# An earlier x, a later W_out and a finer interleave at the start of a convolution and feed-forward kernel

## The chip, the cores and the metric

One core of one Trainium2 chip. Times are device microseconds (us) of one execution; a kernel's figure is the median of its runs. The span of a profile is some 1.75 us shorter than the time of the same execution. All runs here are with a granted TensorE clock of 0.998 or more.

## The reference, cut

```python
# attention part: softmax over 7 taps per head, causal 7-tap convolution along the sequence
out = np.einsum('hk,bskhg->bshg', w, x_unf)      # x: 8 x 4096 x 192, 8 heads of 24 columns
# feed-forward part on the 32768 rows
h = x @ w_in                                     # 192 -> 2048
g = 0.5 * h * (1.0 + erf(h * inv_sqrt2))         # Gelu
return g @ w_out                                 # 2048 -> 192
```

## The kernel before

The two halves of the tokens go side by side through 35 blocks of columns (six of 256, then 29 of 512). For each block DVE transposes x and convolves it, PE does the first layer, ACT the Gelu, PE the second layer. Blocks 0 and 1 are convolved on PE instead, by products with diagonal matrices ("diagonal products"), and their results are copied out of PSUM. W_in comes in three parts (columns 0 to 255, 256 to 511, 512 to 1023 of each half); DVE copies each part to the other half of the partitions. W_out comes in four pieces, cast by GpSimd (POOL in the profile). In blocks 0 and 1 the first layer goes in eight steps (0 to 7), each followed by one Gelu; steps 4 to 7 of block 0 read the copied halves of W_in. Before any data is in, PE runs 16 "warm-up" products on a constant tile.

The parts that the change and the argument touch:

```python
# SyncE: the queue of all later loads
load(sp, 0, (0, 1))            # block 0's x (the other half of it goes on ACT's queue)
sp.wait_ge(S_WIN[0], 32)       # W_in's first part is in
load(sp, 1)                    # block 1's x
for i in range(4):
    ...                        # W_out, four pieces of 384 KB
load(sp, 2)                    # block 2's x
load(sp, 3)
...
# GpSimd: W_in's parts on its own queue; halos; casts of block 1's x; then
for i in range(4):
    g.wait_ge(S_WOUT[i], 16)
    g.tensor_copy(wout[...], woutf[...]).then_inc(S_WOG)      # cast of a piece of W_out
...
# DVE
for p in range(NP): trans(0, p)
conv_out(v, 0, 1); conv_out(v, 0, 4)      # two of block 0's six result copies
dup(0); dup(1)                            # W_in's parts to the other partitions
for p in range(NP): trans(1, p)           # waits for block 1's x
dup(2)
for j in range(len(PIECES)): conv_out(v, 1, j)    # block 1's six result copies
# then for every block from 2 on: three transposes, 21 convolution steps
...
# PE: diagonal products of block 1, behind first-layer steps 4 and 5 of block 0
behind = {
    (0, 4): [(1, kd, k) for k in taps for kd in (0, 1)],
    (0, 5): [(1, kd, k) for k in taps for kd in (2, 3)],
}
```

## Time and profile before

| | before |
|---|---|
| median of the first three runs | 683.88 us (683.34 to 684.79) |
| span of the profile, PE busy in it | 681.6, 675.0 us |
| block 1's x in, transposed from | 12.39, 12.41 us |
| last part of W_in in, last piece of W_out in | 10.70, 18.17 us |
| block 2's x in, transposed from | 19.62, 19.65 us |
| block 1 and block 2: first weights of the first layer | 18.01, 29.15 us |

Landings are the last of the 16 to 64 landing records of a transfer. SyncE's queue in order of time, with the start and length of a group of issues:

```profile
6.53 1.82 SPq L329 DMA_DIRECT2D xin<-in_x_dram  x4
8.39 2.10 SPq L878 DMA_DIRECT2D woutf<-in_moe_w_out_dram  x4
10.53 8.72 SPq L329 DMA_DIRECT2D xin<-in_x_dram  x12
```

W_in alone moves 139 GB/s.

### The profile page before, as it was taken

The page shows a single profiled execution, that of the slowest core. Times are in us where ns is not written, and L with a number is a line of the kernel's source. Part 1 is how long each engine was busy: PE and PEld are TensorE (multiplying, and loading weights), DVE is VectorE, ACT ScalarE, POOL GpSimd, SP SyncE. Part 2 cuts the span into 40 slices and gives each one's busy share as a digit, 9 for nine tenths or more (in the row PEclk, how much of TensorE's full clock was granted, in tenths as well). Part 3 has the DMA queues.
Part 4 walks back from the last instruction along what each step waited for, and adds up shares of the span by engine and source line. Part 5 has one row for each costly group of instructions (what it writes and reads, how often), then busy time and mean ns, then how long its engine had stood idle before and what let it go on. Part 6 is the DMA issues. An engine that isn't in the chain of part 4 may idle for free.

```text
span 681.6 us, 27317 instructions
## 1 busy us (share of the span) xinstructions
PE 675.0 (99%) x12576; PEld 410.1 (60%) x12576; DVE 561.0 (82%) x904; ACT 537.3 (79%) x550; POOL 38.9 (6%) x57
## 2 busy tenths in 40 slices
PE   8999999999999999999999999999999999999998
PEld 4899655555555555555555555555555555555556
DVE  6899979888889888899888898888898888988611
ACT  6899988787787777787777788777878777878772
POOL 5026000000000000000000000000000000000000
PEclk9999999999999999999999999999999999999999
DMA  9446323234332244332244422334322434310123
GB/s 222 86 101 134 79 60 75 43 75 95 96 94 58 45 91 94 95 86 47 60 94 95 94 69 46 78 94 96 94 52 46 95 94 96 83 42 21 48 49 94
DMA packets 132994, 54.79 MB, mean 80 GB/s; under 512 B 126480, under 2 KB 132752, under 8 KB 132880
## 3 DMA queue, kind: packets, MB, share of 16 engines
q1 hardware_dynamic: 130960, 51.50, 32.5%
q8 instruction: 98, 1.61, 1.0%
q0 software_dynamic: 1248, 0.79, 0.9%
q10 hardware_dynamic: 672, 0.76, 0.4%
q14 instruction: 16, 0.13, 0.1%
HBM read 28.66 MB, written 25.17 MB: 79 GB/s over the span
## 4 chain that ended last, share of the span: by engine, by line
PE 96%; ACT 2%; DMA 1%; issue 0%; DVE 0%; SPq 0%; ACTq 0%
PE hp L760 48%; PE ob L824 43%; PE ob L791 6%; ACT gT L681 2%; DMA xin<-in_x_dram 1%; PE ob L711 0%; ACT xc L191 0%; ACT osb L269 0%; DVE osb L311 0%; DVE xT L526 0%; ACT xTb L630 0%; SPq L872 0%; DVE osb L280 0%; SPq L329 0%; ACTq L629 0%
## 5 line engine op out<-in xcount | busy, mean ns | idle before, releaser
L681 ACT ACTIVATE gT<-hp 128x1024 bf16<-128x1024 f32 x512 | 523.3, 1024 | 128.8 <-PE hp L760 125.5
L760 PE MATMUL hp<-xc,win 64*64 64x512 bf16 (+2 forms) x6048 | 419.5, 366 | 1.5 <-ACT gT L681 0.7
L824 PE MATMUL ob<-gT,wout 64*64 64x512 bf16 x5376 | 366.3, 376 | 0.0
L559 DVE SCALAR_TENSOR_TENSOR acc<-xT,wcol,acc 128x512 f32<-128x512 f32 (+1 forms) x495 | 314.1, 698 | 0.0
L760 PEld LDWEIGHTS hp<-xc,win 64*64 64x64 bf16 (+1 forms) x6048 | 189.9, 106 | 134.8 <-ACT gT L681 2.5
L824 PEld LDWEIGHTS ob<-gT,wout 64*64 64x64 bf16 x5376 | 172.3, 118 | 122.8
L311 DVE STREAM_TRANSPOSE osb<-ob 128x512 f32<-128x512 f32 x84 | 74.1, 885 | 100.8 <-PE ob L824 100.8
L526 DVE STREAM_TRANSPOSE xT<-xin 128x512 f32<-128x512 f32 (+1 forms) x105 | 78.6, 797 | 3.8 <-DMA xin<-in_x_dram 3.8
L559 DVE SCALAR_TENSOR_TENSOR xc<-xT,wcol,acc 128x512 bf16<-128x512 f32 (+1 forms) x99 | 65.0, 708 | 0.0
L447 POOL COPY xT<-xT 128x18 f32<-128x18 f32 x30 | 27.9, 930 | 505.2 <-DVE xT L526 482.9
L791 PE MATMUL ob<-wout,gT 64*128 64x192 bf16 x1024 | 52.9, 243 | 0.3
L791 PEld LDWEIGHTS ob<-wout,gT 64*128 64x128 bf16 x1024 | 44.9, 94 | 5.2 <-PE ob L791 0.6
L552 DVE TENSOR_SCALAR acc<-xT,wcol 128x512 f32<-128x512 f32 (+1 forms) x90 | 37.5, 474 | 1.1
L282 ACT ACTIVATE osb<-ob 128x192 f32<-128x192 f32 x4 | 1.3, 332 | 9.5 <-PE ob L791 9.5
L280 DVE COPY osb<-ob 128x192 f32<-128x192 f32 x4 | 1.4, 358 | 8.4 <-PE ob L791 8.4
L695 PE MATMUL hp<-warm 128*128 128x512 bf16 x16 | 5.1, 485 | 1.3 <-DVE warm L463 1.3
L269 ACT ACTIVATE osb<-ob 128x384 f32<-128x384 f32 x12 | 5.8, 486 | 0.0
L654 ACT ACTIVATE acc<-xT,wcol 128x256 f32<-128x256 f32 (+1 forms) x9 | 5.2, 575 | 0.0
L695 PEld LDWEIGHTS hp<-warm 128*128 128x128 bf16 x16 | 1.8, 119 | 4.0 <-issue 1.9
L384 POOL DMA_DIRECT2D win<-in_moe_w_in_dram x6 | 3.9, 658 | 0.8 <-POOLq L905 0.8
L711 PE MATMUL ob<-xTb,dg 64*64 64x256 bf16 (+1 forms) x112 | 3.2, 245 | 0.7 <-ACT xTb L630 0.7
L193 DVE CAST xc<-ob 64x256 bf16<-64x256 f32 (+3 forms) x8 | 2.8, 357 | 1.3 <-PE ob L711 1.1
(31 smaller groups left out, 22.4 us busy)
## 6 DMA issues: line engine op xcount, KB each, us to landing
out_dram<-osb SPq DMA_DIRECT2D x122, 192.0 KB, 3.1
xin<-in_x_dram SPq DMA_DIRECT2D x116, 192.0 KB, 4.1
xin<-in_x_dram SPq DMA_DIRECT2D x20, 96.0 KB, 4.2
woutf<-in_moe_w_out_dram SPq DMA_DIRECT2D x4, 384.0 KB, 6.2
win<-in_moe_w_in_dram POOLq DMA_DIRECT2D x4, 96.0 KB, 4.6
win<-in_moe_w_in_dram POOLq DMA_DIRECT2D x2, 192.0 KB, 5.1
out_dram<-osb SPq DMA_DIRECT2D x8, 48.0 KB, 1.9
out_dram<-osb ACTq DMA_DIRECT2D x4, 96.0 KB, 1.9
```

Source lines behind the costliest of these rows:

```text
L269: e.activation(out=dst, in_=src, func=AF.Copy).then_inc(S_EVA)
L311: v.transpose(ap(osb[m % 2], j, [[8 * C, 128], [C // 2, TB // 32], [NP, 32]]), bank(ring(m, j)),).then_inc(S_EV)
L447: g.tensor_copy(dst, src).then_inc(S_HALO)
L526: v.transpose(ap(xT[n % 2], p * XW + HX, [[NP * XW, 128], [1, w]]), ap(xin[n % NX], p, [[TB // 32 * DQ, 128], [D if n == 0 else DQ, w // 3 ...
L552: ins = v.tensor_scalar(a, src, wk, None, ALU.mult)
L559: ins = v.scalar_tensor_tensor(dst, src, wk, a, op0=ALU.mult, op1=ALU.add)
L654: a.activation(out=acc[n % 2][:, p * TB : p * TB + w], in_=ap(xT[n % 2], p * XW + HX, [[NP * XW, 128], [1, w]]), func=AF.Copy, scale=wcol[ ...
L681: a.activation(out=ap(gT[n % 2], i * c * 2 * w, dst), in_=ap(hp[u % 2], 0, src), func=AF.Gelu,).then_inc(S_GELU)
L695: t.matmul(hp[1][:, 0:512], warm[:, 0:128], warm[:, :])
L760: ins = t.matmul(hp[u % 2][fo : fo + fw, o : o + w], ap(win, f1, [[NP * F, 64], [2, fw]]), xc[n % 2][r, p * TB : p * TB + w], start=(p == ...
L791: ins = t.matmul(bank(bb[sub], w=C), gT[m % 2][r, c0 : c0 + 128], wout[r, CH[sub][i] * C : (CH[sub][i] + 1) * C], start=(ph == 0 and i == ...
L824: ins = t.matmul(bank(ring(m, j), slice(64 * h, 64 * h + 64), w), ap(wout, 64 * hf * NF * C + CH[h][i] * C + j, [[NF * C, 64], [NP, 64]],) ...
```

## The change

Its intent is to have block 1's x early, so that its diagonal products can lie in the slack of block 0's Gelus, and to keep W_out away from the parts of W_in that are needed first.

```diff
@@ DVE @@
-                v.wait_ge(S_WIN[s], 32)
+                v.wait_ge(S_WIN[min(s, 2)], 32)
 ...   (each dup copies a quarter, FQ columns, of a half; before: FQ, FQ, 2 FQ)
+            v.wait_ge(S_TR, NP)
+            v.tensor_copy(<third part of block 0's xTb>, <xT>).then_inc(S_CASTV)
             conv_out(v, 0, 1)
             conv_out(v, 0, 4)
-            dup(0)
-            dup(1)
             for p in range(NP):
                 trans(1, p)
-            dup(2)
-            for j in range(len(PIECES)):
+            for s in range(3):
+                dup(s)
+            for j in range(3):
+                conv_out(v, 1, j)
+            dup(3)
+            for j in range(3, len(PIECES)):
                 conv_out(v, 1, j)
@@ ACT @@
-            for p in range(NP):
+            for p in range(NP - 1):          # casts of block 0's x
@@ PE @@
-                (0, 4): [(1, kd, k) for k in taps for kd in (0, 1)],
-                (0, 5): [(1, kd, k) for k in taps for kd in (2, 3)],
+                (0, 3): [(1, kd, k) for k in taps[:4] for kd in (0, 1)],
+                (0, 4): [(1, kd, k) for k in taps[4:] for kd in (0, 1)],
+                (0, 5): [(1, kd, k) for k in taps[:4] for kd in (2, 3)],
+                (0, 6): [(1, kd, k) for k in taps[4:] for kd in (2, 3)],
 ...   (block 0's products of the third part now wait for S_CASTV)
-                if n == 0 and 4 <= i < 7:
+                if n == 0 and i >= 4:
                     t.wait_ge(S_DUPE, 2 * (i - 4) + 2)
@@ SyncE @@
             load(sp, 0, (0, 1))
-            sp.wait_ge(S_WIN[0], 32)
             load(sp, 1)
+            sp.wait_ge(S_WIN[1], 32)
             for i in range(4):               # W_out
```

More of the change, by code (lines that the diff above doesn't have):

```diff
@@ L148, in bass_lightweight_conv__then__act_gelu_exact_kernel @@
         S_CAST = [sem("S_CAST%d" % i) for i in range(len(PC))]
+        S_CASTV = sem("S_CASTV")
         S_PC = sem("S_PC")
@@ L504, in dup @@
                             win,
-                            64 * (1 - hf) * NP * F + FH + FP[s],
-                            [[NP * F, 64], [F, NP], [1, FP[s + 1] - FP[s]]],
-                        ),
-                        ap(
-                            win,
-                            64 * hf * NP * F + FP[s],
-                            [[NP * F, 64], [F, NP], [1, FP[s + 1] - FP[s]]],
-                        ),
+                            64 * (1 - hf) * NP * F + FH + FQ * s,
+                            [[NP * F, 64], [F, NP], [1, FQ]],
+                        ),
+                        ap(win, 64 * hf * NP * F + FQ * s, [[NP * F, 64], [F, NP], [1, FQ]]),
                     ).then_inc(S_DUPE)
@@ L581, in _ @@
                 trans(0, p)
+            v.wait_ge(S_TR, NP)
+            v.tensor_copy(
+                ap(xTb[0], (NP - 1) * XB + HL, [[NP * XB, 128], [1, WS[0]]]),
+                ap(xT[0], (NP - 1) * XW + HX, [[NP * XW, 128], [1, WS[0]]]),
+            ).then_inc(S_CASTV)
             conv_out(v, 0, 1)
             conv_out(v, 0, 4)
-            dup(0)
-            dup(1)
             for p in range(NP):
                 trans(1, p)
-            dup(2)
-            for j in range(len(PIECES)):
+            for s in range(3):
[4 more added lines that the diff above has]
+            for j in range(3, len(PIECES)):
                 conv_out(v, 1, j)
@@ L700, in pconv @@
                 if k == KS - 1:
-                    t.wait_ge(S_CAST[PC[n]], p + 1)
+                    if n == 0 and p == NP - 1:
+                        t.wait_ge(S_CASTV, 1)
+                    else:
+                        t.wait_ge(S_CAST[PC[n]], p + 1)
                     if n == 0:
```

## The prediction

> **What bounds the kernel now.** I read the page first, for the share of each engine, then the chain that ended last, then the start in order of time, because the diff touches nothing after block 1.
>
> ```profile
> span 681.6 us, 27317 instructions
> PE 675.0 (99%) x12576; PEld 410.1 (60%) x12576; DVE 561.0 (82%) x904; ACT 537.3 (79%) x550; POOL 38.9 (6%) x57
> ...
> PE 96%; ACT 2%; DMA 1%; issue 0%; DVE 0%; SPq 0%; ACTq 0%
> ```
>
> The first lines are the busy times, the last is the chain of waits by engine. PE carries 96% of the chain, so the time can change only by what is not PE: 681.6 - 675.0 = 6.6 us in all, of which 5.93 us pass before the first x is transposed and nothing in the diff shortens that. The whole room of the change is therefore well under 2% (13.7 us).
>
> Next the start in order of time (start, length, engine, line; in brackets the idle time ahead and its releaser), cut to the lines that decide:
>
> ```profile
> 12.41 1.34 DVE L526 STREAM_TRANSPOSE xT<-xin 128x256 f32<-128x256 f32 x3 [1.57 <-DMA xin<-in_x_dram]
> 13.89 0.96 PE L711 MATMUL ob<-xTb,dg 64*64 64x256 bf16 x28
> 15.54 0.59 PE L711 MATMUL ob<-xTb,dg 64*64 64x128 bf16 x28
> 15.65 1.02 ACT L681 ACTIVATE gT<-hp 128x1024 bf16<-128x1024 f32 x1 [0.63 <-PE hp L760]
> 15.81 2.29 DVE L193 CAST xc<-ob 128x256 bf16<-128x256 f32 x6
> 16.93 4.00 ACT L681 ACTIVATE gT<-hp 128x1024 bf16<-128x1024 f32 x4 [0.26 <-PE hp L760]
> 18.22 0.83 POOL L457 CAST wout<-woutf 128x768 bf16<-128x768 f32 x1 [1.25 <-DMA woutf<-in_moe_w_out_dram]
> 19.65 1.35 DVE L526 STREAM_TRANSPOSE xT<-xin 128x256 f32<-128x256 f32 x3 [1.54 <-DMA xin<-in_x_dram]
> 21.82 6.02 DVE L559 SCALAR_TENSOR_TENSOR acc<-xT,wcol,acc 128x256 f32<-128x256 f32 x15
> 27.77 1.26 DVE L559 SCALAR_TENSOR_TENSOR xc<-xT,wcol,acc 128x256 bf16<-128x256 f32 x3
> 29.14 0.58 PEld L760 LDWEIGHTS hp<-xc,win 64*128 64x128 bf16 x12 [0.15 <-issue]
> ```
>
> See three things. (1) From 10.10 to about 18 us ACT's Gelu sets the pace of block 0, and the two lumps of 28 diagonal products put gaps of 0.63 and 0.26 us into it. (2) Block 1's first layer starts at 18.01 us (its weights in the trace), behind a Gelu and behind the six copies that DVE ends at 18.10. (3) Block 2's x lands only at 19.6 us: DVE idles 1.54 us for it, then works without a hole, and its last convolution step ends at 29.03; block 2's first weights load at 29.15. So PE is handed block 2 0.12 us after DVE ends. The stretches from that landing on show DVE full:
>
> ```profile
> 19.65:29.10 9.45, 9.32 (x196) 8.32 (x192) 9.41 (x25) 7.35 (x9) 0.31 (x1) 1.00 0.27 52
> 29.10:39.70 10.60, 10.60 (x228) 10.53 (x225) 10.56 (x28) 9.61 (x14) 0.39 (x2) 1.00 0.34 85
> ```
>
> The columns are the length, then busy time of PE, PEld, DVE, ACT, POOL, the clock, the DMA share and GB/s. DVE is busy 9.41 of 9.45 and 10.56 of 10.60 us: it is as full as PE. I set the end of each block's last convolution step beside the first weight load of that block, from the same trace: block 2 29.03 and 29.15, block 3 39.56 and 39.67, block 4 47.92 and 50.14, block 5 57.33 and 60.66, block 6 69.26 and 71.18, and 2.1 us apart or more from there to the end. So up to 39.7 us the true chain runs: landing of block 2's x, then 19.9 us of DVE work, then PE. The page's chain names PE there because PE is also busy; the two are almost tied, with PE's slack about 0.15 us at block 2 and 0.06 at block 3.
>
> **What the Trainium skill says.** "DMA: Bandwidth & Descriptors", section "Queues, rings and completion order": each DMA engine takes turns between the queues that have work for it, and takes one queue's work in order. The trace agrees: W_in is on POOL's queue, everything else on SP's, W_out's packets come behind block 1's x. The page's "Specifications" table puts line rate at 512 B and up; x's rows here are 384 B packets. The trace shows about 300 of them in 0.5 us (230 GB/s) with two blocks of x in flight, against 350 GB/s while W_out's 1536 B packets run (11.5 to 15.0 us), so it agrees in direction. "Perfetto Trace Analysis", "Identifying the Most-Contended Engine": matmul busy time says little, weight-load busy time more; here PEld is 8.32 of 9.45 us in block 1 and 10.53 of 10.60 in block 2, so it doesn't hide a large hole either. "VectorE: DVE Perf Modes", section "The perf-mode tier table", bears on the one cast moved to DVE; no row of the trace has that very shape.
>
> **The change part by part.**
> The cast of block 0's third part goes from ACT (0.417 us) to DVE, an estimate of 0.3 to 0.4 us from the 0.42 us that a 256-wide copy out of PSUM takes. The part is transposed at 7.26; ACT's cast ended at 7.72, DVE's will at about 7.6. But the first copies of block 0's result start at 8.01 and wait for earlier products. Gain: 0 to 0.1 us.
> The slots: 28 + 28 products become 16, 12, 16, 12 behind the first-layer steps 3 to 6. The lumps took 0.89 and 0.52 us of PE; a slot takes 0.51, 0.38, 0.30, 0.22. A step of 0.66 to 0.83 us plus a slot nearly fits a Gelu of 1.02, so of the 0.89 us of gaps I expect 0.1 to 0.3 to remain. The six copies start at 14.4 instead of 15.8; the last three (0.29 + 0.29 + 0.28) follow the last slot at about 16.4, or W_in's last copy (two of 0.42), and end at 17.4. Block 1 then starts at 17.4 in place of 18.0: 0.6 us gained on PE.
> The copies of W_in's other half: 4 of 0.42 and 2 of 1 us become 8 of 0.42, the same work, now ahead of the wait by need only.
> The orders of transfers: block 1's x is issued at 2.1 us rather than at 6.53, and W_out when W_in's second part is in rather than at 8.39. Bytes are unchanged. Block 1's x lands at some 8 to 10 us instead of 12.39, which the slots need (first one at 12.8).
> What it does to block 2's x decides. Before, between 7.0 and 8.75 us W_in ran alone at 139 GB/s; with x beside it, 8.75 to 11.5, the engines moved 251. So putting x into the earlier stretch saves up to (251 - 139) x 1.75 = 196 KB, an estimate of 0.6 to 0.8 us. Against it, W_out is now issued at 7.6 to 9.2 us (W_in's second part: 31 of 32 engine landings by 7.4 us before, one straggler at 8.71), and its first packets came 2 us after issue. That is 9.7 to 11.2 us, against 10.4 before (but then at half rate until 12). Shift of W_out and hence of block 2's x: between -0.9 and +0.4 us, most likely -0.4.
> Sum: the end moves by the smaller gain of the two chains, min(0.6 + 0.15 on PE, 0.4 on DVE's) = 0.4 us. 683.88 - 0.4 = about 683.5.
>
> **The rivals.**
> A: the PE gain counts in full, 0.6 us or more, 683.2. For it: the page's chain is nearly all PE. Against: the 0.12 us hand-overs at blocks 2 and 3, which swallow what isn't matched by an earlier x.
> B: the gain is lost entirely; block 2's x lands where it did, as the same bytes go through the same engines ahead of it, and PE merely waits longer at 29 us: 683.9. For it: DMA share is 0.94 to 1.45 from 4.5 to 19.65 us. Against: the thin stretch at 7 us.
> C: W_out starts late, a hole opens between W_in's end and W_out's start, and block 2's x comes 0.5 to 1 us late: 684.4 to 684.9. For it: the new wait is on the queue that carries all later x as well, and it hangs on the slowest of 32 landings.
> D: W_in's last part, now sharing with x, lands after 11.2 us, where step 2 needs it (10.70 before), or W_in's first part after 8.85 (6.51 before). Slack 0.5 and 2.3 us; a miss costs PE a few tenths, which the 0.6 us would absorb.
>
> **Range and chances.** I weigh my path 45%, B 25%, C 20%, A 10%; runs of the kernel before already spread from 683.34 to 684.79, and I take that spread to come from landings such as these. Predicted 683.5 us, 8 in 10 between 682.6 and 684.6. More than 2% either way is out of reach of a change that touches 20 us: faster 0.5%, within 2% 98.5%, slower 1%.
>
> **What would show it.** Block 1's transposes before 11 us: x early, right. Gelu gaps of block 0 under 0.3 us and block 1's first layer near 17.4: slots, right. Then block 2's transposes: their start against 19.65 should equal the shift of its last convolution step (29.03), of block 3's hand-over (39.67) and of the end. If the transposes start no earlier and PE has a wait of 0.5 us or more at 29 us, B is right; a start later than 19.8 means C. I'd be wrong at the root if the end moves without the transposes moving, or if the DVE chain has holes after them. If the end moves by over 1 us, the cause lies outside block 2's landing, and I have missed a part.

## More of the kernel before

The columns are the stretch and its length, the busy time of PE, PEld (weight loads), DVE, ACT and POOL, then the clock, the DMA share and GB/s:

```profile
7.00:8.75 1.75, 1.68 (x56) 1.47 (x56) 0.66 (x3) 1.43 (x4) 0.76 (x3) 1.00 0.94 139
13.00:15.00 2.00, 1.87 (x44) 1.41 (x46) 1.94 (x4) 1.99 (x3) 1.98 (x4) 1.00 1.09 383
```

W_out, from 13 to 15 us, moves 383.

## The result, and the profile after

| | before | after |
|---|---|---|
| median, four runs each | 683.71 us (683.34 to 684.79) | 684.69 us (683.96 to 685.62) |
| ratio, 95% interval | | 1.0012 (0.9995 to 1.0030) |
| span of the profile | 681.6 | 683.0 |

A ratio is the mean time of one kernel's runs over that of the other's of the same rounds, so it is not quite the ratio of the medians. The verdict is "same" at 2%, as predicted; the predicted gain of 0.4 us isn't there, and the changed kernel tends to be about 1 us slower. Its median lies 0.09 us above the top of the stated range, the ratio times 683.71 (684.5) just inside.

The page of the changed kernel, busy times and chain:

```profile
span 683.0 us, 27320 instructions
PE 676.3 (99%) x12576; PEld 410.3 (60%) x12576; DVE 562.0 (82%) x907; ACT 536.4 (79%) x549; POOL 38.8 (6%) x57
...
PE 95%; ACT 2%; DVE 1%; DMA 1%; issue 0%; SPq 0%
```

PE's busy time rose by 1.3 us, though it does the same 12576 products. The 16 warm-up products alone take 6.59 us instead of 5.05 (more on them below). The start in order of time:

```profile
9.76 1.94 SPq L887 DMA_DIRECT2D woutf<-in_moe_w_out_dram  x4
10.80 1.34 DVE L523 STREAM_TRANSPOSE xT<-xin 128x256 f32<-128x256 f32 x3 [1.20 <-DMA xin<-in_x_dram]
12.17 3.77 DVE L503 COPY win<-win 64x768 bf16<-64x768 bf16 x6
15.98 1.33 DVE L194 CAST xc<-ob 128x256 bf16<-128x256 f32 x3
17.34 0.87 DVE L503 COPY win<-win 64x768 bf16<-64x768 bf16 x2
18.36 1.49 PE L769 MATMUL hp<-xc,win 64*128 64x256 bf16 x24 [0.73 <-DVE win L503]
19.23 2.98 ACT L685 ACTIVATE gT<-hp 128x1024 bf16<-128x1024 f32 x3 [0.82 <-PE hp L769]
21.07 1.34 DVE L523 STREAM_TRANSPOSE xT<-xin 128x256 f32<-128x256 f32 x3 [2.02 <-DMA xin<-in_x_dram]
30.57 0.47 PEld L769 LDWEIGHTS hp<-xc,win 64*128 64x128 bf16 x10 [0.30 <-issue]
```

Block 1's x is transposed at 10.80 instead of 12.41. But block 2's transposes start at 21.07 instead of 19.65, 1.42 us later, and the span is 1.42 us longer. PE, at block 2, stands idle for 0.30 us. It too is late: the first Gelu of block 0 starts at 10.86 (10.10 before), the fourth pair of W_in copies (17.34) stands behind result copies and holds up first-layer step 7 of block 0, with a Gelu gap of 0.82 us behind it, and block 1 starts at 18.90 instead of 18.01. The stretches of the changed kernel:

```profile
7.00:8.75 1.75, 1.75 (x45) 1.12 (x47) 0.89 (x3) 0.64 (x2) 1.14 (x4) 1.00 1.30 225
13.00:15.00 2.00, 2.00 (x44) 1.30 (x44) 1.94 (x3) 1.75 (x2) 1.60 (x2) 1.00 0.88 232
```

From 7 to 8.75 us the engines move 225 GB/s instead of 139: the gain that the prediction counted on. From 13 to 15 they move 232 instead of 383. In that stretch almost nothing but W_out is on the engines in either kernel: 487 of its packets start before, 292 after, with a median of 0.065 us in both. So most packets are not slower; there are fewer of them. What was won is lost again, and more.

### The profile page after: what moved, and what is told of

Its sections match the earlier page's. It is cut to its first block, busy times and chain, and to the rows that moved or that the text cites. A ratio compares the mean times of both kernels' runs of the same rounds, so it can differ in the third digit from the quotient of the medians.

```text
span 683.0 us, 27320 instructions
## 1 busy us (share of the span) xinstructions
PE 676.3 (99%) x12576; PEld 410.3 (60%) x12576; DVE 562.0 (82%) x907; ACT 536.4 (79%) x549; POOL 38.8 (6%) x57
## 4 chain that ended last, share of the span: by engine, by line
PE 95%; ACT 2%; DVE 1%; DMA 1%; issue 0%; SPq 0%
PE hp L769 47%; PE ob L833 42%; PE ob L800 5%; ACT gT L685 1%; DMA xin<-in_x_dram 1%; DVE win L503 1%; SPq L330 0%; DVE xT L523 0%; DVE xc L194 0%; ACT osb L270 0%; DVE osb L312 0%; SPq L881 0%; DVE osb L281 0%
## 5 line engine op out<-in xcount | busy, mean ns | idle before, releaser
L699 PE MATMUL hp<-warm 128*128 128x512 bf16 x16 | 6.6, 604 | 1.3 <-DVE warm L464 1.3
L503 DVE COPY win<-win 64x768 bf16<-64x768 bf16 x8 | 4.5, 558 | 0.2
```

The source lines that it names most:

```text
L503: v.tensor_copy(ap(win, 64 * (1 - hf) * NP * F + FH + FQ * s, [[NP * F, 64], [F, NP], [1, FQ]],), ap(win, 64 * hf * NP * F + FQ * s, [[NP ...
L699: t.matmul(hp[1][:, 0:512], warm[:, 0:128], warm[:, :])
```

## The experiments

Theory ("chains"): the end is set by the later of two chains, landing of block 2's x plus DVE's work, and PE's own work; both slipped. Rivals for the late landing: W_out released late; chance; DVE's copies or GpSimd's casts disturbing the transfers; the slots. The first table has all results; the second has what the profiles show. Kernels are compared only within the same rounds. "Late" release means W_out behind W_in's second part, "early" behind its first.

| run | edit, against the changed kernel (A) or before (B) | median, before | ratio (95%) |
|---|---|---|---|
| e0 | A again | 684.57, 683.57 | 1.0015 (1.0002 to 1.0027) |
| e1 | A with the transfer order of B | 686.68, 683.57 | 1.0047 (1.0034 to 1.0060) |
| e2 | B with the transfer order of A | 683.62, 683.57 | 1.0000 (0.9988 to 1.0013) |
| e3 | A, fourth W_in copy ahead of block 1's result copies | 684.04, 683.57 | 1.0003 (0.9990 to 1.0017) |
| e4 | A, casts of W_out held until all of it is in | 687.48, 683.91 | 1.0049 (1.0027 to 1.0071) |
| e5 | A, W_in copies cut to 16 columns (wrong result) | 684.95, 683.91 | 1.0015 (0.9998 to 1.0031) |
| e6 | e2 again | 684.60, 683.58 | 1.0016 (1.0002 to 1.0030) |
| e7 | A without the slots | 684.01, 683.58 | 1.0010 (0.9997 to 1.0022) |
| e8 | e3, W_out behind W_in's first part | 684.26, 683.58 | 1.0008 (0.9995 to 1.0020) |
| e9 | e8, casts held as in e4 | 684.78, 683.46 | 1.0012 (0.9998 to 1.0026) |
| e10 | A, W_out behind W_in's first part | 684.10, 683.46 | 1.0006 (0.9993 to 1.0019) |
| e11 | e2, W_out behind W_in's first part | 684.02, 683.46 | 1.0005 (0.9993 to 1.0018) |

| profile | block 1's x | W_out | GB/s, 13 to 15 us | W_out's last piece in | block 2's x in | its transposes | span less that | PE idle ahead of block 2 |
|---|---|---|---|---|---|---|---|---|
| before | second | early | 383 | 18.2 | 19.62 | 19.65 | 661.96 | 0.15 |
| e1 | second | early | 383 | 17.7 | 19.37 | 20.93 | 663.69 | none |
| after | first | late | 232 | 19.9 | 21.04 | 21.07 | 661.97 | 0.30 |
| e0 | first | late | 204 | 19.3 | 20.84 | 20.87 | 661.96 | 0.56 |
| e2 | first | late | 292 | 18.2 | 19.58 | 19.60 | 662.03 | none |
| e3 | first | late | 215 | 20.1 | 21.29 | 21.32 | 661.98 | 0.46 |
| e4 | first | late | 205 | 19.7 | 20.92 | 20.95 | 664.75 | none |
| e5 | first | late | 258 | 20.0 | 21.28 | 21.30 | 661.96 | 0.43 |
| e6 | first | late | 240 | 19.0 | 20.45 | 20.47 | 661.97 | 0.72 |
| e7 | first | late | 243 | 20.1 | 21.37 | 21.40 | 661.97 | 0.54 |
| e8 | first | early | 361 | 15.6 | 18.77 | 19.26 | 663.23 | none |
| e9 | first | early | 366 | 17.9 | 19.49 | 19.52 | 663.57 | none |
| e10 | first | early | 355 | 17.8 | 19.48 | 19.51 | 662.77 | none |
| e11 | first | early | 342 | 15.9 | 19.09 | 19.11 | 663.17 | none |

Read the last three columns first. Wherever PE idles ahead of block 2, the span is the start of block 2's transposes plus 661.96 to 661.98 us, in seven profiles of six kernels. Wherever PE doesn't idle there, the span is longer than that sum: then PE is the later chain (e2 is the tie, 662.03). This holds for every profile, so the end is read off two numbers at 20 to 30 us. (The last column is the idle time of PE's weight loads, as in the line at 30.57 above.)

**e0, the changed kernel again.**

> The changed kernel again, unchanged, for its spread and a second profile. Chain theory (the end is the start of block 2's transposes plus 661.9 us, as 19.65 gave 681.6 before and 21.07 gave 683.0 after): the span of this profile is its own transposes' start plus 661.9 within 0.2. Rival, chance: block 2's x lands anywhere from 19.5 to 21.5 in any run and the mean against before is within 0.3 us. Rival, the order itself: landing again at 20.7 or later and the mean 0.7 to 1.3 us slower than before.

684.57 against 683.57, landing at 20.84, span 682.8 = 20.87 + 661.96. The slower time is there a second time, with an interval that leaves out 1.0. Its spread is wide, though (683.86 to 685.66).

**e1 and e2, one half of the change each.**

```diff
 e1: A with                              e2: B with
-            load(sp, 1)                 -            sp.wait_ge(S_WIN[0], 32)
-            sp.wait_ge(S_WIN[1], 32)                  load(sp, 1)
+            sp.wait_ge(S_WIN[0], 32)    +            sp.wait_ge(S_WIN[1], 32)
+            load(sp, 1)
```

> The changed compute order (slots, split copies, moved cast) with the transfer order of before. If the new transfer order is what delays block 2's x: landing back at about 19.6, end set by the later of DVE chain and PE; x of block 1 is back at 12.4, so the W_in copies on DVE come after it, 12.4 + 1.35 + 6 x 0.45 to 0.9 = 17 or later, and first-layer steps 4 to 7 of block 0 wait for them: PE slow by about 1 to 2 us, total 684.5 to 685.5. If chance alone made the difference: same as before within 0.3.

> The compute order of before with only the new transfer order. If the transfer order is to blame for all: block 2's x lands at 20.7 or later and the end is 0.7 to 1.4 us later than before (684.4 to 685.1). If W_out's late issue is not the cause but the lagging engines are chance: landing near 19.6 on average and the end within 0.3 of before.

e1 was 3.1 us slower than before, twice what I expected. The landing is back, at 19.37, but DVE is free for it only at 20.93, and PE is later still:

```profile
12.64 1.33 DVE L523 STREAM_TRANSPOSE xT<-xin 128x256 f32<-128x256 f32 x3 [3.60 <-DMA xin<-in_x_dram]
14.00 3.81 DVE L503 COPY win<-win 64x768 bf16<-64x768 bf16 x6
15.02 0.83 PE L769 MATMUL hp<-xc,win 64*128 64x256 bf16 x12 [0.31 <-DVE win L503]
20.22 1.49 PE L769 MATMUL hp<-xc,win 64*128 64x256 bf16 x24 [1.14 <-DVE win L503]
```

These lines are from the order of time of e1: DVE idles 3.60 us for block 1's x with all its W_in copies queued up behind, and PE waits for the copies. The new compute order can't do without the early x.

e2 looked the same as before, and its profile had block 2's x at 19.58. Taken alone this says that the new transfer order is harmless and the compute order guilty. It is the one look that misled me; e6 contradicts it.

**e3, the copy that PE waits for moved ahead.**

```diff
-            for s in range(3):
-                dup(s)
-            for j in range(3):
-                conv_out(v, 1, j)
-            dup(3)
-            for j in range(3, len(PIECES)):
-                conv_out(v, 1, j)
+            for s in range(4):
+                dup(s)
+            for j in range(len(PIECES)):
+                conv_out(v, 1, j)
```

> The changed kernel with the fourth W_in copy moved ahead of block 1's result copies, so that first-layer step 7 of block 0 doesn't wait for it behind them. Chain theory with x2 as the bound: Gelu gap of 0.82 ahead of step 7 goes, block 1 starts some 0.4 to 0.7 us earlier, but the end stays with block 2's transposes: same as the changed kernel within 0.3. If PE's late start is the bound: 0.5 us or more faster than the changed kernel.

The gap went, as both theories said: block 1 starts at 17.91. From the fourth to the eighth Gelu of block 0 it now takes 4.69 us, against 4.99 before, so slots without the copy's delay are worth 0.3 us. The median is 0.53 us under e0's. By the letter that is the second expectation (0.5 us or more, PE's late start is the bound), but by 0.03 us, while each kernel's five runs spread over 1.5 us or more, so e3's times alone do not decide. In its profile block 2's x is the bound: it is in at 21.29, and the span is the transposes' start plus 661.98. That profile is of e3's slowest run, though (685.08; the others 683.53 to 684.16), so it shows this for one run only. And it shows a second harm of the late W_out. This line is from its order of time:

```profile
21.06 0.83 PE L797 MATMUL ob<-wout,gT 64*128 64x192 bf16 x16 [1.13 <-POOL wout L458]
```

PE, early at block 1, waits 1.13 us for the last casts of W_out. In this run the late transfers hold back both chains.

**e4 and e5, is it GpSimd's casts or DVE's copies that slow the transfers?** Both overlap the stretch from 13 to 15 us.

```diff
 e4: GpSimd
             for i in range(4):
                 g.wait_ge(S_WOUT[i], 16)
+            for i in range(4):
                 o = 2 * WG[i] * C
 e5: DVE
+            <zero W_in's copied half early, v.wait_ge(S_MSW, 2) ahead of each dup>
-                            [[NP * F, 64], [F, NP], [1, FQ]],
+                            [[NP * F, 64], [F, NP], [1, 16]],
```

> The changed kernel, but GpSimd's four casts of W_out wait until all of W_out has landed. In the runs with the slots, W_out's rate falls from about 245 packets per us to 100 to 170 between 13 and 15 us, from about half a us after the first of these casts. Theory casts: with GpSimd quiet W_out keeps its rate, its last part lands at 17 or earlier (19.3 and 19.9 in the two profiles of the changed kernel) and block 2's x at 19.8 or earlier; the casts then end at 20.3 or so and first keep PE waiting, so the end is 683 to 685. Theory of the W_in copies on DVE, or of chance or lock-step among the engines: the fall at 13 us stays, W_out's last part at 19 or later, x at 20.7 or later.

> The changed kernel with the eight copies of W_in's other half cut to 16 of 256 columns (its result is wrong on purpose; that half is zeroed early by DVE). If DVE's copies slow the transfers: W_out's last part lands at 18 or earlier and block 2's x at 19.8 or earlier, the end 1 us earlier than the changed kernel. If they only hold up DVE and through it PE: first-layer steps 4 to 7 of block 0 start up to 1.5 us earlier, W_out and x land as in the changed kernel (19.3 and 20.8 or later), and the end stays within 0.3 us of it. They collide with GpSimd's casts (0.42 us alone, 0.80 to 0.97 beside a cast); that disappears in any case.

Neither. With GpSimd idle from 13 to 15 us the engines move 205 GB/s, without DVE's copies 258, and block 2's x lands at 20.92 and 21.28. (e4's end is 3.6 us late because PE waits 2.71 us for the casts, which I had put at 683 to 685. e5's early zeroing put its first diagonal products at 8.68 us, so only its transfers may be read.)

**e6 and e7, the transfer order once more, and the slots.** e6 is e2's code; e7 is A with `behind` as in B.

> The kernel before with only the new transfer order, a second time, for a second profile. If the transfers of this order are slow by themselves and the first profile (x of block 2 at 19.58) was luck: landing at 20.5 or later here and a median 0.5 us or more above before. If the late landing needs the new compute order as well: landing at 20.2 or earlier, median within 0.3 us of before, as the first time.

> The changed kernel with the diagonal products of block 1 back in two lumps of 28; transfers, split W_in copies and moved cast stay. If the slots are what makes block 2's x late: landing at 20.2 or earlier. If the order of DVE's work is: 20.7 or later as in the five profiles of the changed order. Gelu gaps of 0.6 us at step 5 return; the result copies of kinds 0 to 2 still stand ahead of the fourth W_in copy, so step 7 still waits: end 684.3 to 685.3 if late, 683.6 to 684.6 if not.

e6's stretch from 13 to 15 us, and its transposes of block 2:

```profile
13.00:15.00 2.00, 1.77 (x44) 1.26 (x44) 1.36 (x2) 1.99 (x3) 1.81 (x3) 1.00 0.93 240
20.47 1.35 DVE L526 STREAM_TRANSPOSE xT<-xin 128x256 f32<-128x256 f32 x3 [3.13 <-DMA xin<-in_x_dram]
```

e6 is 1.02 us slower than before, with the landing at 20.45: the transfer order can be slow by itself, on the code of before. e2's five runs at 683.36 to 683.96 and e6's at 684.18 to 685.40 do not overlap; why the same code did better in one (the two were on different chips) stays open. It was not one lucky run: no profile has its span less than 661.96 us after the start of block 2's transposes, so e2's five spans (681.6 to 682.2) put that start at 20.3 or earlier in all five. e7 lands at 21.37 without the slots. So casts, copies and slots, each taken away alone, leave the landing late, and the transfer order remains as the suspect; how much it costs differs.

**e8, e10, e11: W_out released earlier, all else as in e3, the changed kernel, and e2.**

```diff
             load(sp, 1)
-            sp.wait_ge(S_WIN[1], 32)
+            sp.wait_ge(S_WIN[0], 32)
```

> The changed kernel with the fourth W_in copy first and W_out's transfers let go when W_in's first part is in (about 7.6 us) rather than its second (9.5). If the wait for the second part makes W_out and block 2's x late (a hole in the engines' work at 10 to 11 us): W_out's packets start by 9.7, its last part lands before 18.5 and x before 20, and the end is at 683.5 or earlier unless W_in's last part, now sharing, lands after 11.5 and stalls step 2. If the engines' falling apart after 13 us is the cause: stragglers in W_out as before, x at 20.5 or later, the end at 684 or later.

> The changed kernel with nothing else but W_out let go behind W_in's first part instead of its second. If that wait is the cause of the late landing: W_out's last part by 16.5 and block 2's x by 19.2; the end then hangs on DVE's copies as in the run with the fourth copy first, or worse by the two copies behind block 1's result copies: 683.6 to 684.8. If the tight landings of that run were luck: W_out's last part at 18 or later, x at 20.4 or later.

> The compute order of before, block 1's x first and W_out behind W_in's first part: the new transfer order without its second wait. If that wait is the cause: W_out's last part by 16.5, block 2's x by 19.2, and since PE of the old compute order is ready for block 2 only at 29.0, the end is 0 to 0.4 us earlier than before (683.2 to 683.6) and PE no longer waits there. Otherwise as in the two runs of the new order: 683.6 to 684.6.

The stretch from 13 to 15 us of e10:

```profile
13.00:15.00 2.00, 2.00 (x46) 1.24 (x44) 1.94 (x3) 1.95 (x3) 1.07 (x2) 1.00 1.07 355
```

and of e11:

```profile
13.00:15.00 2.00, 1.58 (x42) 1.20 (x40) 1.36 (x2) 1.99 (x3) 2.00 (x4) 1.00 1.11 342
```

Three kernels, one edited word each, and 355, 342 and 361 GB/s (e10, e11, e8) in place of 204 to 232, 240 to 292 and 215. Block 2's x lands at 18.77 to 19.48. Over all profiles the split is complete: eight with the late release have 204 to 292 GB/s there, six with the early one (before and e1 among them) 342 to 383. Each pair that differs by one word comes from two calls, on different chips; within the two calls that have both kinds the split is the same (383 in e1 beside 204 to 292 in e0, e2 and e3; 361 in e8 beside 240 and 243 in e6 and e7). The late wait is the cause of the slow stretch from 13 to 15 us. Over 13 to 17 us the two groups nearly touch (247 to 279 and 281 to 306), and the landings of block 2's x just overlap (19.58 to 21.37 and 18.77 to 19.62): the rate falls every time, the delay that comes of it varies. What it does is not a plain late start: the first two pieces of W_out land at 12.9 and 13.9 in the changed kernel, 0.8 us ahead of before. Then the sixteen engines fall apart; the third piece lands at one after the other from 14.5 to 18.2, in e8 at all from 14.2 to 14.5. (e8 is the neatest: that piece's landings spread over 0.3 to 2.1 us in the six early profiles, over 2.1 to 4.1 in the eight late ones.)

The times do not follow. e10 and e11 are 684.10 and 684.02, against 683.46 for before, each a little slower than before with intervals that hold 1.0, and PE doesn't idle at block 2 in either: now PE is late. For e10, the chain of waits in order of time (start, length, what):

```profile
5.20 6.36 DMA win<-in_moe_w_in_dram
11.55 0.14 issue
11.69 1.49 PE hp L769 x24
...
16.87 1.03 ACT gT L685
17.90 0.83 PE hp L769 x12
18.73 0.02 issue
18.75 1.03 ACT gT L685
```

It starts from W_in's last part, which lands at 11.55 (10.70 before, where x came beside it only from about 8.7 us on) and is needed at 11.17 before, at about 11.4 here, where the first Gelu starts 0.22 us later; the third Gelu is 0.29 us later still. And the fourth copy delays step 7 again: the chain names a Gelu there, but step 7 needs only the Gelu before that one, while the copy ends at 17.74 and the weights start 0.12 us later, as in the changed kernel (18.21 and 18.33). In e11, which has neither slots nor the moved copy, W_in's last part lands at 11.42, and PE's weight loads then stand 0.78 us inside step 7 for nothing that the trace shows (0.36 before, 0.28 in e0, 0.37 in e7, 0.72 in e8; in no other profile). One 16 KB instruction fetch goes over the same DMA engines a little earlier: in these five profiles the pause ends 1.3 to 1.6 us after it, and in four of them (not before) the fetch ends at 16.6 to 17.0 us, later than in all the others. That points to the fetch, but nothing was tried. e11's prediction of 683.2 to 683.6 was a miss; these two are what its trace shows late, and neither was tested alone.

**e9, an attempt at a better version.** e8's pace from 11 to 19 us is set by DVE. In order of time:

```profile
11.15 5.75 DVE L503 COPY win<-win 64x768 bf16<-64x768 bf16 x8
16.93 2.30 DVE L194 CAST xc<-ob 128x256 bf16<-128x256 f32 x6
19.26 0.94 DVE L523 STREAM_TRANSPOSE xT<-xin 128x256 f32<-128x256 f32 x2
```

Eight copies of 0.42 us alone are 3.4 us with no gap to speak of. Four of them take 0.80 to 1.02 us, each beside a cast on GpSimd. The Trainium skill, "SBUF — State Buffer", section "Who interferes with whom", says that DVE in its two-port modes and GpSimd share one pair of ports, and that the second to start is blocked until the first is done. The trace agrees: 0.42 us alone, up to 1.09 beside a cast of 0.83 (e10). So e9 holds the casts back, as e4 does, with the early W_out.

> The run with the fourth W_in copy first and W_out behind W_in's first part, with GpSimd's casts of W_out held until all of W_out is in (15.6 us in its profile). There DVE's copies and result copies set the pace from 9.78 to 19.28 us, four of the eight W_in copies taking 0.80 to 1.02 us beside a cast instead of 0.42. Chain theory: copies at 0.42 us each, the six result copies done by 17.6, block 1 at 17.7 or earlier, block 2's transposes at 18.8 (its landing), span 680.7 to 681.2, time 682.4 to 682.9, that is 0.7 to 1.2 us faster than before. Against: the four casts end at 18.9 and PE waits for them in block 1; then 683.0 to 683.8.

```profile
11.52 3.58 DVE L504 COPY win<-win 64x768 bf16<-64x768 bf16 x8
18.09 3.14 POOL L459 CAST wout<-woutf 128x768 bf16<-128x768 f32 x4 [6.03 <-DMA woutf<-in_moe_w_out_dram]
19.75 0.51 PE L798 MATMUL ob<-wout,gT 64*128 64x192 bf16 x8 [0.65 <-POOL wout L459]
21.29 0.83 PE L798 MATMUL ob<-wout,gT 64*128 64x192 bf16 x16 [0.38 <-POOL wout L459]
```

The copies take 3.58 us, so that step is right, though block 1 starts at 18.26, not by 17.7. But W_out's last piece lands at 17.9 in this run, not 15.6, the four casts end at 21.2, and PE waits for them twice. 684.78: a miss, worse than "against" in its own expectation. No version beat the kernel before.

## Why the prediction was right or wrong

- What bounds the kernel: right, and the sharpest part. (A slip without effect: not all but W_in is on SP's queue; half of block 0's x comes on ACT's.) Seven profiles have the span at the transposes' start plus 661.96 to 661.98 us where PE idles at block 2. In the profile pair of the change, start and span both moved by 1.42 us.
- The class and the chances: right. Nothing in 20 us of start could move 2%.
- The sum, -0.4 us: wrong in sign. The step that failed is the one named "Shift of W_out and hence of block 2's x: between -0.9 and +0.4 us, most likely -0.4". Measured in the profiles of the changed kernel: +1.42 and +1.22; over the eight late-release profiles -0.04 to +1.75. The term for x in the thin stretch was about right (225 GB/s where I had estimated up to 251), and with the early release, x first, block 2's x lands 0.1 to 0.9 us sooner than before. What I mis-sized is the new wait. I weighed only its delay of the first packets (9.7 to 11.2 us; measured 10.79, from an issue at 9.76 where I had 9.2 at the latest). That alone hurt nothing, as W_out's first two pieces were early. I had no term for a slower rate after 13 us.
- Rival C, given 20%, is what happened to the landing, in another way than written: not as "a hole between W_in's end and W_out's start" (W_out's first pieces were early) but as engines falling apart two pieces later.
- The signs named in advance: block 1's transposes before 11 us came true (10.80), and block 2's later than 19.8 (21.07) say C. The Gelu gaps under 0.3 us did not (0.82 at step 7). The last sign, "If the end moves by over 1 us, the cause lies outside block 2's landing", was wrong: the span moved by 1.42 us, and block 2's landing by the same.
- The 0.6 us for PE: wrong. Block 1 starts 0.89 us later in the first profile and 0.44 in the second, not 0.6 earlier. The terms: the slots are worth 0.3 us (e3), not 0.6; "or W_in's last copy" was a remark where it should have been the bound, for the copies took 0.97 us beside casts, where I counted 0.42 for all, and pushed step 7 to 18.3; x of block 0 landed at 6.24 instead of 5.91, sharing with block 1's x (5.98 to 6.38 in all twelve profiles with x first, 5.89 and 5.91 in the other two); and PE's warm-up products ran at half pace until 7.2 us instead of 4.2.
- The warm-up looks like chance, not the change. Its products' spacing goes from 0.427 to 0.216 us at some point, and that point lay between 4.1 and 5.9 us in the other profiles, with 5.8 in e0, the same kernel, and 4.6 and 5.9 in e2 and e6, one kernel. "TensorE: Matmul & The Clock Gate", section "Part 1: The HAM clock gate", of the Trainium skill puts this down to a free-running window, so that the point varies from run to run; the trace agrees that it varies, though by more than the half microsecond either way given there.
- Rival D, W_in's last part late, was real (11.03 to 11.58 with the late release, 11.32 to 11.87 with the early one and x first). I expected the 0.6 us on PE to absorb it; there was no such gain, and in e10 it heads the chain.
- The moved cast: 0.29 us on DVE, where 0.3 to 0.4 was estimated, and no effect seen.

Two kernels' difference of about 1 us is smaller than the spread within one kernel (683.86 to 685.66 in e0). That the changed kernel is slower at all rests on e0, e6 and the landings, not on single times. Not settled: by what the late release makes the engines fall apart after 13 us. W_out is issued at 7.4 to 8.5 us in the early releases and at 9.3 to 9.8 in the late ones, so SyncE has less of a lead over the engines. That lead is my guess, not shown. Slow packets don't tell the two apart: one or two of W_out's 1024 take 0.9 to 1.5 us where 0.07 is usual in every late release, but one does before (1.55) and in e9 (1.26) too. Casts, copies and slots, taken away one at a time, are not needed for it. Open too is the rest of the slowdown: with the early release e10 is still 0.64 us above before (its interval holds 1.0), by W_in's late part and the fourth copy as its trace has it. The first was not tested alone, and moving the copy ahead as well (e8, 684.26) gained nothing.

## What to carry to other kernels

When a profile's main engine is at 99%, look for the hand-overs where a second engine is just as full, and find the one early event that both hang on; here it was one landing at 19.6 us, and every later time is that plus a constant. A wait put on a queue delays not only the transfer behind it but everything later on that queue, so price it at the last transfer that hangs on it, over several profiles. Repeat a half of a change before acquitting it: e2 said "harmless", e6 said "the cause".

## What the Trainium skill lacked or had wrong

- "DMA: Bandwidth & Descriptors" has nothing on how far ahead of the engines a queue has to be issued. With W_out issued at 9.3 to 9.8 us instead of 7.4 to 8.5, the engines moved 204 to 292 GB/s instead of 342 to 383 from 13 to 15 us, and the third piece's sixteen landings spread over 2.1 to 4.1 us instead of 0.3 to 2.1. That it is the lead is a guess.
- The same page says that issuing from several engines doesn't help bandwidth, as all run on the same sixteen DMA engines. That lacks the case of a stream that alone moves less than they can: W_in alone moved 139 GB/s, and the engines 225 with x's 384-byte packets, from another queue, between its own. No run put x on W_in's queue, so it isn't shown that the second queue is what helps.
- The same page, section "Queues, rings and completion order", has engines take turns between queues, but gives no figure for the delay of one stream by another: W_in's last part landed at 10.70 us when x came later, and at 11.2 to 11.9 in eleven of the twelve profiles with x first (11.03 in e2).
- "TensorE: Matmul & The Clock Gate", section "Part 1: The HAM clock gate", puts the scatter of the warm-up's end at about 0.5 us either way. Here it lay between 4.1 and 7.2 us over fourteen profiles. A note in the same section, that one kernel had 6, 11 or 14 slow products, fits better: here 7 to 14.
- I found on no page a size for PE's pauses with no wait in the trace: 0.28 to 0.78 us inside one first-layer step, in five of fourteen profiles.
